# Loading the first weight block of a fused mixer kernel in column halves on two queues

## The chip, the cores and the metric

The kernel runs on one core of a Trainium2 chip. The metric is device time in microseconds (us). The kernel before takes 206.7 us (206.62 to 207.2 in three executions). In the views of the profile PE is TensorE, PEld its weight loads, DVE VectorE, ACT ScalarE, POOL GpSimd and SP SyncE; a trailing q marks a queue's issue of a load. A load has "landed" when its completion is signalled.

## The reference, cut to what matters

Two mixers work on the same `x` (2048 x 512) and are blended by a gate of each row. The change touches only the beginning of branch B: `x @ w_in`, of which the second half of the columns goes through a gelu and a layer norm.

```python
def _B_ref(x, w_in, w_sp, b_sp, w_out):
    z = _gelu(jnp.einsum('bsd,df->bsf', x, w_in))     # w_in is 512 x 1376
    z1 = z[..., :Fh].copy()
    z2 = _layernorm(z[..., Fh:], axis=-1)             # Fh = 688: the kernel starts here
    g = jnp.einsum('ts,bsf->btf', w_sp, z2) + b_sp[None, :, None]
    return jnp.einsum('bsf,fd->bsd', z1 * g, w_out)
g = _sigmoid((x * gate_w).sum(-1, keepdims=True))     # gate: one more column of z2's product
a = _A_ref(x, A_wqkv, A_w_phi, A_wo)                  # linear attention; ... cut
b = _B_ref(x, B_w_in, B_w_sp, B_b_sp, B_w_out)
return g * a + (1 - g) * b
```

## The kernel before

The 512 rows of `w_in` are four blocks of 128 rows; here "block 0" to "block 3" are their z2 columns (128 x 688 bf16, 172 KB each). SP and ACT each have a queue of loads.

```python
def load_z2w(eng, dt):
    eng.dma_start(out=w_z2[:, dt, 0:FH], in_=w_in_v[:, dt, FH:F])
nc.sync.dma_start(out=xs[:, 0, :], in_=x2[0:P, :])          # first two x tiles
nc.scalar.dma_start(out=xs[:, 1, :], in_=x2[P:2 * P, :])
load_z2w(nc.sync, 0)
load_z2w(nc.scalar, 1)
load_z2w(nc.sync, 2)
nc.scalar.dma_start(out=gaterow[0:NDT, :], in_=gate_w.rearrange("(dt p) -> dt p", p=P))
load_z2w(nc.sync, 3)
# ... cut
x_dma_T(2, 2)                    # first DMA transpose on SP: x tiles 2 and 3
# ... cut: w_z1 (2 loads), further x tiles (transposed), brow, wqkT (transposed)
for u in range(8):
    nc.sync.dma_start(out=wphi[us, :, us], in_=heads[u])    # needed by fold()
# ... cut: wv_sb (2 loads), wspT (transposed)
```

TensorE (PE) starts with warm-up matmuls on constants, transposes two x tiles, and then runs the z2 products of both tiles, in the order in which their blocks are expected.

```python
warm_up(6); warm_up(1, P)
# ... cut: eight transposes of x tiles 0 and 1, copies to xT
one(0, 0, 0)                 # one(tile, block, column half)
z_part(0, 0, HF, True)       # tile 0, block 0, second half
gate_T()                     # transposes gaterow; needs its load
one(0, 1, 0)                 # first use of block 1
one(1, 0, 0)
z_part(1, 0, HF, True)
one(1, 1, 0)
# ... cut: blocks 1 (second half), 2 and 3 of both tiles
```

The softmax here doesn't subtract the row's maximum and nothing guards it: scores larger than these inputs give would overflow.

## Time and profile before

| What | Where it is read | Value |
|---|---|---|
| span of the profiled execution | page | 204.5 us |
| PE busy | page, part 1 | 98% |
| first z matmul | timeline of PE | 4.53 us |
| block 1 issued / landed after | issues of the tile | 1.24 us / 3.4 us |
| first DMA transpose on SP issued | timeline of SP | 2.66 us |
| last `w_phi` load issued | timeline of SP | 23.96 us |
| fold, first to last matmul | timeline of PE | 25.93 to 26.41 us |

The page of the kernel before: busy us of each engine with its share of the span, and the engines of the chain of work that ended last.

```profile
PE 200.8 (98%) x1557; PEld 119.9 (59%) x1557; DVE 130.4 (64%) x283; ACT 74.8 (37%) x122; POOL 45.6 (22%) x76
...
PE 98%; DVE 0%; issue 0%
```

PE is the bound from end to end, so only a wait of PE can be won or lost. The timeline of PE around the first z matmuls (start us, length us, engine, line, operation, out<-in, count):

```profile
4.10 0.42 PE L280 MATMUL pq<-ident,xs 128*128 128x128 bf16 x2
4.53 0.44 PE L191 MATMUL zp<-w_z,xT 128*128 128x344 bf16 x1
4.77 0.38 PE L230 MATMUL zp<-w_z,xT 128*128 128x344 bf16 x1
4.99 0.17 PE L290 MATMUL pq<-ident,gaterow 128*128 128x4 bf16 x1
5.02 0.45 PE L191 MATMUL zp<-w_z,xT 128*128 128x344 bf16 x2
5.31 0.31 PE L230 MATMUL zp<-w_z,xT 128*128 128x344 bf16 x1
5.46 0.89 PE L191 MATMUL zp<-w_z,xT 128*128 128x344 bf16 x5
```

Look at the starts, for the lengths overlap. The last transpose starts at 4.21, and the first z matmul only at 4.53: about 0.2 us of waiting for block 0. From 5.02 on a z matmul starts each 0.145 us, without a gap.

The same time from the SP queue (timeline of SP; its rows are issues of loads), with the `w_phi` row far below:

```profile
0.81 0.39 SPq L119 DMA_DIRECT2D xs<-in_A_x_dram  x1
1.25 1.36 SPq L117 DMA_DIRECT2D w_z<-in_B_w_in_dram  x3
2.66 1.33 SPq L131 DMA_TRANSPOSE xT<-in_A_x_dram  x1
4.04 1.08 SPq L135 DMA_DIRECT2D w_z<-in_B_w_in_dram  x2
...
20.25 4.13 SPq L150 DMA_DIRECT2D wphi<-in_A_w_phi_dram  x8
```

SP issues without a pause: the transpose goes out the moment the load before it is issued. The last of the eight `w_phi` loads goes out at 23.96. It landed 1.6 us later, at 25.56, and the fold starts at 25.93:

```profile
25.93 0.56 PEld L307 LDWEIGHTS <-wqkT 32*128 32x128 bf16 x64 [0.28 <-issue]
```

That is no wait, but under 0.4 us of slack; I did not see this before I predicted. Two more views are compared below: the stretches from 3.5 to 4.5 us (last two columns: busy share of the DMA engines, which can pass 1 because a packet counts whole where it starts, and GB/s; before them the busy time of each engine and the granted clock), and the issue of block 1 with its time to landing.

```profile
3.50:4.00 0.50, 0.50 (x8) 0.50 (x7) 0.19 (x1) 0.32 (x2) 0.00 (x0) 1.00 0.97 302
4.00:4.50 0.50, 0.50 (x5) 0.36 (x4) 0.40 (x3) 0.00 (x0) 0.00 (x0) 1.00 0.98 312
```

```profile
L117 ACTq DMA_DIRECT2D w_z<-in_B_w_in_dram x1: 456/456/456, 1.2 to 1.2; - x1
...
DMA to landing us min/median/max: 3.4/3.4/3.4
```

### The profile page before, as it was taken

To read this page: it belongs to the slowest core of one execution; us is meant where nothing else is said; L and a number is where in the kernel's file an instruction comes from. 1 tells how busy PE (TensorE), PEld (TensorE's weight loads), DVE (VectorE), ACT (ScalarE), POOL (GpSimd) and SP (SyncE) were. 2 spreads that over 40 slices of the span, in tenths; PEclk is the share of its full clock that TensorE was granted. 3 is DMA by queue.
4 is the path that set the end of the run, shared out by engine and by line. 5 is a ranking of instruction groups with operands and counts; after the bars stand their busy time and mean duration, and the time that the engine had idled before them with its cause. 6 is when DMAs were issued, how large, how long until landed. Compare 5 with 4: busy or idle time off the path is not lost.

```text
span 204.5 us, 3996 instructions
## 1 busy us (share of the span) xinstructions
PE 200.8 (98%) x1557; PEld 119.9 (59%) x1557; DVE 130.4 (64%) x283; ACT 74.8 (37%) x122; POOL 45.6 (22%) x76
## 2 busy tenths in 40 slices
PE   8999999999999999999999999999999999999994
PEld 4666666655665555656565666555555555665642
DVE  4567484837977587979797789555566645633332
ACT  3566678796222333332424042222251136002303
POOL 3020202021523325334242442222204220200000
PEclk9999999999999999999999999999999999999999
DMA  6999699999999027940423219853567458552833
GB/s 194 252 205 171 80 151 290 146 278 247 256 249 213 3 38 182 287 94 16 75 48 45 51 38 120 154 109 64 105 161 80 90 113 183 63 96 51 156 64 104
DMA packets 89931, 27.22 MB, mean 133 GB/s; under 512 B 84184, under 2 KB 89912, under 8 KB 89912
## 3 DMA queue, kind: packets, MB, share of 16 engines
q1 hardware_dynamic: 87744, 24.99, 65.4%
q10 hardware_dynamic: 2168, 1.98, 3.5%
q8 instruction: 12, 0.20, 0.4%
q14 instruction: 7, 0.06, 0.1%
HBM read 4.15 MB, written 2.10 MB: 31 GB/s over the span
## 4 chain that ended last, share of the span: by engine, by line
PE 98%; DVE 0%; issue 0%
PE mm L454 37%; PE zp L191 18%; PE mm L355 14%; PE mm L515 9%; PE mm L509 7%; PE mm L395 7%; PE kvacc L411 2%; PE at L467 2%; PE zp L222 1%; PE mm L520 1%; PE zp L307 0%; PE pq L280 0%; PE at L478 0%; PE pq L307 0%; DVE ob L527 0%; PE zp L230 0%
## 5 line engine op out<-in xcount | busy, mean ns | idle before, releaser
L454 PE MATMUL mm<-z2all,wspT 128*128 128x344 bf16 x512 | 79.9, 309 | 0.0
L454 PEld LDWEIGHTS <-wspT 128*128 128x128 bf16 x512 | 49.0, 98 | 25.3
L191 PE MATMUL zp<-w_z,xT 128*128 128x344 bf16 (+1 forms) x254 | 38.1, 310 | 0.0
L359 ACT ACTIVATE eq<-mm 128x512 bf16<-128x512 f32 x32 | 17.4, 594 | 51.4 <-PE mm L355 25.7
L363 DVE TENSOR_REDUCE zs<-eq 128x64 f32<-128x1024 bf16 x16 | 19.5, 1220 | 20.0 <-ACT eq L359 20.0
L191 PEld LDWEIGHTS <-xT 128*128 128x128 bf16 x254 | 24.4, 98 | 11.8
L359 ACT ACTIVATE ek<-mm 128x512 bf16<-128x512 f32 x32 | 17.3, 600 | 27.1 <-PE mm L355 27.1
L459 DVE SCALAR_TENSOR_TENSOR ucat<-mm,bT,z1all 128x344 bf16<-128x344 f32 x32 | 17.4, 544 | 15.0 <-PE mm L454 15.0
L372 POOL TENSOR_TENSOR eq<-eq,ratio 128x512 bf16<-128x512 bf16 x16 | 16.9, 1055 | 44.6 <-DVE ratio L371 36.7
L531 ACT ACTIVATE ob<-mm,g_inv 128x512 bf16<-128x512 f32 (+1 forms) x15 | 10.1, 680 | 33.1 <-PE mm L520 28.5
L363 DVE TENSOR_REDUCE zs<-ek 128x64 f32<-128x1024 bf16 x16 | 19.3, 1209 | 2.8 <-ACT ek L359 2.8
L515 PE MATMUL mm<-wspT,uT 128*128 128x512 bf16 (+2 forms) x85 | 20.1, 367 | 0.0
L355 PEld LDWEIGHTS <-xT 128*128 128x128 bf16 x128 | 12.2, 98 | 12.0
L372 POOL TENSOR_TENSOR ek<-ek,ratio 128x512 bf16<-128x512 bf16 x16 | 16.9, 1056 | 2.2 <-DVE ratio L371 1.7
L509 PE MATMUL mm<-wspT,oT 128*128 128x512 bf16 (+2 forms) x68 | 16.6, 366 | 0.0
L355 PE MATMUL mm<-wq_p,xT 128*128 128x512 bf16 x64 | 16.4, 379 | 0.0
L395 PE MATMUL mm<-wv_sb,xT 128*128 128x512 bf16 x64 | 16.4, 379 | 0.0
L355 PE MATMUL mm<-wk_p,xT 128*128 128x512 bf16 x64 | 16.3, 379 | 0.0
L209 DVE BATCH_NORM_STATS2 bn<-z2all 128x6 f32<-128x344 bf16 x32 | 14.9, 501 | 0.0
L206 ACT ACTIVATE z2all<-zp 128x688 bf16<-128x688 f32 x16 | 11.8, 744 | 7.3 <-PE zp L191 7.2
L260 ACT ACTIVATE z1all<-zp 128x688 bf16<-128x688 f32 x16 | 11.9, 744 | 5.1 <-PE zp L191 4.6
L515 PEld LDWEIGHTS <-uT 128*128 128x128 bf16 x85 | 8.1, 98 | 9.4 <-issue 0.2
(77 smaller groups left out, 142.7 us busy)
## 6 DMA issues: line engine op xcount, KB each, us to landing
out_dram<-ob ACTq DMA_DIRECT2D x12, 128.0 KB, 2.4
wspT<-in_B_w_out_dram SPq DMA_DIRECT2D x2, 640.0 KB, 4.9
w_z<-in_B_w_in_dram SPq DMA_DIRECT2D x2, 344.0 KB, 4.7
w_z<-in_B_w_in_dram SPq DMA_DIRECT2D x3, 172.0 KB, 3.5
wv_sb<-in_A_wqkv_dram SPq DMA_DIRECT2D x2, 256.0 KB, 2.7
wspT<-in_A_wo_dram SPq DMA_DIRECT2D x2, 256.0 KB, 4.0
out_dram<-ob SPq DMA_DIRECT2D x3, 128.0 KB, 1.8
uT<-ucat SPq DMA_TRANSPOSE x16, 2.8
```

Of the source, the lines that this page charges most:

```text
L191: nc.tensor.matmul(zp[:, j, 0:n], lhsT=xT[:, dt, tt * P:(tt + 1) * P], rhs=wt[:, dt, j * HF:j * HF + n], start=(dt == 0), stop=(dt == NDT ...
L209: nc.vector.bn_stats(out=bn6[:, tt, j, :], in_=z2v[:, j, :])
L260: nc.scalar.activation(out=z1all[:, tt, :].rearrange("p (j n) -> p j n", j=2), in_=zp[:, :, 0:HF], func=AF.Gelu_apprx_tanh,)
L355: nc.tensor.matmul(ps[:, :], lhsT=xT[:, dt, tt * P:(tt + 1) * P], rhs=w[:, dt, :], start=(dt == 0), stop=(dt == NDT - 1))
L359: nc.scalar.activation(out=e[:, :, a, :], in_=ps[:, :].rearrange("p (h f) -> p h f", f=DH), func=AF.Exp, scale=1.0 - 2.0 * a)
L363: nc.vector.tensor_reduce(out=z[:].rearrange("p h a -> p (h a)"), in_=e[:].rearrange("p h a f -> p (h a) f"), axis=AX.X, op=ALU.add,)
L372: nc.gpsimd.tensor_tensor(out=e[:, :, 1, :], in0=e[:, :, 1, :], in1=ratio[:, :, None].to_broadcast([P, H, DH]), op=ALU.mult)
L395: nc.tensor.matmul(v_ps[:, :], lhsT=xT[:, dt, tt * P:(tt + 1) * P], rhs=wv_sb[:, dt, :], start=(dt == 0), stop=(dt == NDT - 1))
L454: nc.tensor.matmul(gp[:, 0:HF], lhsT=wspT[:, st, tt * P:(tt + 1) * P], rhs=z2all[:, st, j * HF:(j + 1) * HF], start=(st == 0), stop=(st == ...
L459: nc.vector.scalar_tensor_tensor(out=ucat[tt % NU][:, c0 + j * HF:c0 + (j + 1) * HF], in0=gp[:, 0:HF], scalar=bT[:, tt:tt + 1], in1=z1all[ ...
L509: nc.tensor.matmul(acc, lhsT=oTs[tt][:, g, :], rhs=wo_t[:, g, c0:c1], start=start and g == 0, stop=stop and g == NG - 1)
L515: nc.tensor.matmul(acc, lhsT=uTs[tt][:, i + ft, :], rhs=w_main[i][:, ft, c0:c1], start=start and ft == 0, stop=False)
```

## The change

Block 0 is cut into two column halves of 344, one on each queue right behind the x tiles, so that it no longer shares the engines with block 1 (in the kernel before they landed at 4.49 and 4.68 us, and from 3.5 to 4.0 us the SP queue moved 0.05 MB and the ACT queue 0.10). PE uses block 0 for both tiles before it needs the gate row and block 1. The two loads of `wv_sb` become one.

```diff
-    load_z2w(nc.sync, 0)
+    for eng, c in ((nc.sync, 0), (nc.scalar, HF)):
+        eng.dma_start(out=w_z2[:, 0, c:c + HF], in_=w_in_v[:, 0, FH + c:FH + c + HF])
     load_z2w(nc.scalar, 1)
@@
-    for h in range(2):
-        nc.sync.dma_start(
-            out=wv_sb[:, 2 * h:2 * h + 2, :],
-            in_=A_wqkv[h * 2 * P:(h + 1) * 2 * P, 2 * D:3 * D].rearrange("(dt p) n -> p dt n", p=P),
-        )
+    nc.sync.dma_start(out=wv_sb[:, :, :], in_=A_wqkv[:, 2 * D:3 * D].rearrange("(dt p) n -> p dt n", p=P))
@@
         one(0, 0, 0)
         z_part(0, 0, HF, True)
+        one(1, 0, 0)
+        z_part(1, 0, HF, True)
         gate_T()
         one(0, 1, 0)
-        one(1, 0, 0)
-        z_part(1, 0, HF, True)
         one(1, 1, 0)
```

## The prediction

> **What bounds the kernel now.** TensorE: the page gives PE 200.8 of 204.5 us busy (98%), and the chain that ended last is 98% PE. Only at the start can a load hold PE back, so all that the change can win lies in the first 5 us or so.
>
> **The start, from the timeline of the first 8 us.** PE warms up from 0.84 us, then runs eight transposes of two x tiles, one each 0.107 us (128 columns: half speed), the last starting at 4.21 and so feeding until about 4.32. The first z matmul starts at 4.53: the load of w_in block 0, issued at 1.25, took 3.2 us to land. So PE waits about 0.21 us for block 0. It runs the second z matmul at 4.77, the gate matmul at 4.99 (weight load at 4.92, just after gaterow lands), the next z at 5.02, and from there one z each 0.145 us without a gap. Full clock is recorded from 4.92 us on; the waited 0.21 us was half-speed time, worth about 0.10 us at full speed. That is the whole prize: 0.05% of 206.7 us.
>
> **What the change does to it.** In the DMA packet records, block 0 (SP queue) and block 1 (ACT queue) end at nearly the same time (last data 3.97 and 4.23 us): they share the engines[...]. So block 0 is there when about 600 KB have moved. After the change only 256 KB of x and 172 KB of block 0 come first: at some 300 GB/s (packet records of 2.25 to 4.25 us) about 0.5 us earlier, landing near 4.0 (estimate). The first z matmul is then released by the transposes, near 4.32.
>
> The price: block 1 and gaterow sit behind half of block 0 on the ACT queue, behind about 770 KB in all. Estimate: block 1 lands near 5.1 instead of 4.65, gaterow near 5.3 instead of 4.88. PE has four block-0 matmuls to cover this: two at half speed (4.32 to 4.90), two mostly at full speed, done at about 5.20. So the gate matmul stalls up to about 0.1 us, and block 1 is just in time. Sixth z matmul: before at 5.46; after at 5.40 to 5.50. Blocks 2 and 3 come at the same total of bytes as before, and land (5.26, 5.72) before they are needed (5.9, 6.5). Net: 0.0 to 0.1 us won.
>
> The merged load of wv_sb takes one 0.45 us issue from SP at 24.4 us; wv_sb is first used at 45.4. The order of DVE and GpSimd is unchanged; ACT gets one more issue before its table load, whose result is not needed before 7.03.
>
> **Predicted time: 206.6 us, 8 in 10 between 206.2 and 207.1.** Faster by over 2%: 0.01; within 2%: 0.98; slower by over 2%: 0.01.
>
> **What would show it.** Right: first z matmul at 4.3 to 4.4, no longer behind a load; gaterow named as the wait before the gate's weight load; block 1 landing 0.3 to 0.6 us later; the sixth z start within 0.1 us of before; the rest of the PE stream merely shifted. Wrong: block 0 landing after 4.4, or a gap over 0.2 us before the gate or block 1.
>
> **What would make it wrong.** The moment of full clock moves between executions[...]. A lost PE slot late in the kernel would also outweigh it.

The sum comes to 206.7 us less the 0.0 to 0.1 us won at the start, so 206.6. Half speed is what the traces have before the moment of full clock that they record (4.92 us before, 5.96 in the change): z matmuls start 0.29 us apart (4.36 to 4.65 in the change), and 0.145 us after it.

## More of the kernel before

The transposed loads of the later x tiles follow on SP, and far behind them the loads of `w_phi`.

`fold()` later multiplies the attention weights with `w_phi`, on PE, between two z tiles.

In the trace the SP and ACT loads signal their landing on eight semaphores in turn. The ninth load gets the first one's again, and this program makes it wait on it: in the kernel before that is a load of `w_z1`, which goes out at 4.04 us and waits for the load of x tile 1 (landed at 3.58).

## The result, and the profile after

The change takes 207.19 us in the median (206.97 to 207.85, 6 executions), the kernel before 206.66 us (206.58 to 207.2): a ratio of 1.0025, interval 1.0008 to 1.0042. Ratios here are the mean time of one kernel's fast runs over that of the other's of the same rounds, so not quite the ratio of the medians. It is slower clear of noise, by about 0.5 us, and the median is 0.09 us above the predicted range. A second timing (`after_again`, below) gave 207.07 us and again 1.0025. That 207.07 lies inside the predicted range is luck: the same waits are in its profile, and the forecast was a gain of 0.0 to 0.1 us.

The page after: PE is still nearly all of the chain, but loads have come into it.

```profile
PE 200.5 (97%) x1539; PEld 120.0 (58%) x1557; DVE 130.4 (63%) x283; ACT 74.7 (36%) x122; POOL 45.6 (22%) x76
...
PE 94%; DMA 2%; DVE 1%; issue 1%; ACTq 0%; ACT 0%
```

(The trace lacks 18 of the 1557 matmul records; they are missing, not idle.) The timeline of PE at the start of the change, with the wait and its releaser in brackets:

```profile
4.15 0.42 PE L277 MATMUL pq<-ident,xs 128*128 128x128 bf16 x2
4.36 0.49 PE L188 MATMUL zp<-w_z,xT 128*128 128x344 bf16 x1
4.65 0.49 PE L227 MATMUL zp<-w_z,xT 128*128 128x344 bf16 x1
4.94 0.49 PE L188 MATMUL zp<-w_z,xT 128*128 128x344 bf16 x1
5.22 0.49 PE L227 MATMUL zp<-w_z,xT 128*128 128x344 bf16 x1
5.83 0.18 PE L287 MATMUL pq<-ident,gaterow 128*128 128x4 bf16 x1
6.37 1.04 PE L188 MATMUL zp<-w_z,xT 128*128 128x344 bf16 x6 [0.35 <-DMA w_z<-in_B_w_in_dram]
```

The first z matmul starts at 4.36, right after the transposes, as intended. Four block-0 matmuls run. Then PE waits for gaterow until 5.83, and for block 1 until 6.37. In the kernel before the fifth and sixth z matmuls started at 5.31 and 5.46; here at 6.37 and 6.51. Block 1 took this long:

```profile
L117 ACTq DMA_DIRECT2D w_z<-in_B_w_in_dram x1: 454/454/454, 1.7 to 1.7; - x1
...
DMA to landing us min/median/max: 4.6/4.6/4.6
```

Issued at 1.73, landed at 6.33. Much had gone ahead of it. The DMA view up to block 1's last data (5.88 us; in the second profile of the change, `after_again`, 5.11 us) has the total and the two queues, q1 being SP's and q10 ACT's (the last line is the total of the second profile):

```profile
DMA packets 1324, 1.04 MB, mean 177 GB/s; under 512 B 435, under 2 KB 1324, under 8 KB 1324
q1 hardware_dynamic: 885, 0.64, 39.4%
q10 hardware_dynamic: 439, 0.40, 20.1%
...
DMA packets 993, 0.94 MB, mean 183 GB/s; under 512 B 122, under 2 KB 993, under 8 KB 993
```

In the first profile the trace also has fifteen of block 1's sixteen completion signals by 5.63 us and the last only at 6.33; in the second profile no such straggler. The engines also moved less from 3.5 to 4.5 us than before (302 and 312 GB/s there):

```profile
3.50:4.00 0.50, 0.50 (x7) 0.47 (x6) 0.14 (x1) 0.50 (x1) 0.00 (x0) 1.00 0.88 208
4.00:4.50 0.50, 0.50 (x7) 0.50 (x5) 0.41 (x3) 0.32 (x2) 0.00 (x0) 1.00 0.88 267
```

And the SP queue has a pause that was not there before:

```profile
1.73 0.90 SPq L117 DMA_DIRECT2D w_z<-in_B_w_in_dram  x2
3.71 1.33 SPq L132 DMA_TRANSPOSE xT<-in_A_x_dram  x1
5.08 1.08 SPq L136 DMA_DIRECT2D w_z<-in_B_w_in_dram  x2
...
22.59 3.81 SPq L151 DMA_DIRECT2D wphi<-in_A_w_phi_dram  x8
```

The loads before it are issued by 2.63, but the transpose goes out at 3.71 (2.66 before). The compiled program says why. This is SP's queue of the change (a listing of the program, not a profile):

```
1 L119 DMACopy xs<-in_A_x_dram 128x512
2 L122 DMACopy w_z_69<-in_B_w_in_dram 128x344
3 L117 DMACopy w_z_69<-in_B_w_in_dram 128x688 x2
4 L132 DmaTransposeAnt xT<-in_A_x_dram 128x4x256 [waits DMAHW0_49]
```

With one load more ahead of it, the transpose is the ninth and gets the first semaphore again, on which this program makes it wait: that of ACT's load of x tile 1. Before, the transpose was the eighth and waited for nothing. In the trace x tile 1 landed at 3.69 us, and the transpose goes out at 3.71 (second profile: 3.52 and 3.54). The rest of SP's queue starts about 1 us later. At the fold, PE now waits for `w_phi` (timeline of the weight loads):

```profile
26.98 0.10 PEld L304 LDWEIGHTS <-wqkT 32*128 32x128 bf16 x3 [0.28 <-DMA wphi<-in_A_w_phi_dram]
27.68 0.56 PEld L304 LDWEIGHTS <-wqkT 32*128 32x128 bf16 x61 [0.61 <-DMA wphi<-in_A_w_phi_dram]
```

One can add this up by landmarks of the timelines. The table gives each moment in us, and in brackets how far it is behind the kernel before. It has runs that come below.

| Profile | first gelu of z2 | first gelu of z1 | last fold matmul | first exp of k |
|---|---|---|---|---|
| before | 7.03 | 10.82 | 26.41 | 45.95 |
| change | 8.08 (+1.05) | 11.88 (+1.06) | 28.16 (+1.75) | 47.59 (+1.64) |
| change, second profile | 7.49 (+0.46) | 11.61 (+0.79) | 27.38 (+0.97) | 46.81 (+0.86) |
| `lane_only` | 6.98 (-0.05) | 11.11 (+0.29) | 26.76 (+0.35) | 46.19 (+0.24) |
| `lane_again` | 7.13 (+0.10) | 10.93 (+0.11) | 27.98 (+1.57) | 47.40 (+1.45) |
| `halves_sp` | 7.44 (+0.41) | 11.24 (+0.42) | 28.05 (+1.64) | 47.51 (+1.56) |
| `halves01` | 7.00 (-0.03) | 10.80 (-0.02) | 26.50 (+0.09) | 45.92 (-0.03) |

After the fold nothing more is lost: the spans of the two profiles of the change, 206.1 and 205.3 us, are 1.6 and 0.8 us over the 204.5 of before, as the last column says. (The profile of before fell on one of its faster executions, 206.2 us, and the first of the change on its slowest, 207.85 us, so these differences are larger than the 0.5 us of the medians. The second profile, of a 207.06 us execution, is the more usual one.)

### The profile page after: what moved, and what is told of

Read it like the earlier page. It is cut to its first block, busy times and chain, and to the rows that moved or that the text cites. A ratio compares the mean times of both kernels' runs of the same rounds, so it can differ in the third digit from the quotient of the medians.

```text
span 206.1 us, 3978 instructions
## 1 busy us (share of the span) xinstructions
PE 200.5 (97%) x1539; PEld 120.0 (58%) x1557; DVE 130.4 (63%) x283; ACT 74.7 (36%) x122; POOL 45.6 (22%) x76
## 4 chain that ended last, share of the span: by engine, by line
PE 94%; DMA 2%; DVE 1%; issue 1%; ACTq 0%; ACT 0%
PE mm L451 36%; PE zp L188 18%; PE mm L352 13%; PE mm L512 8%; PE mm L392 7%; PE mm L506 7%; DMA w_z<-in_B_w_in_dram 2%; PE kvacc L408 2%; PE at L464 2%; PE mm L517 1%; DVE bn L206 0%; ACT z2all L203 0%; PE zp L304 0%; PE at L475 0%; PE pq L304 0%
## 5 line engine op out<-in xcount | busy, mean ns | idle before, releaser
L506 PE MATMUL mm<-wspT,oT 128*128 128x512 bf16 (+2 forms) x61 | 15.6, 364 | 0.4
```

What stands on the lines that cost most here:

```text
L506: nc.tensor.matmul(acc, lhsT=oTs[tt][:, g, :], rhs=wo_t[:, g, c0:c1], start=start and g == 0, stop=stop and g == NG - 1)
```

## The experiments

Theories. **G**: block 1 and gaterow are late behind half of block 0, and PE waits for them. **L**: the ninth load waits for a semaphore, the SP queue is late, and PE waits later, at the first z1 tile and at the fold. **H**: a gap in PE's work at the start delays the full clock. All kernels gave correct results. "before" is the kernel before in the same rounds.

### First round: the parts one by one

`reorder_only`: the loads of before, the matmul order of the change.

> The loads of the kernel before, the matmul order of the change (gate matmul after the four block-0 matmuls of both tiles). All theories: nothing, within 0.1 us of before (206.66), because block 1 lands at 4.65 us and is never waited for. If the reorder alone cost time, the ratio would be over 1.001.

Measured: 206.26 us (206.11 to 206.78), before 206.43; ratio 0.9995, interval 0.9979 to 1.0011. The order alone does nothing that this timing can show.

`halves_only`: the change with the matmul order of before.

```diff
-        one(1, 0, 0)
-        z_part(1, 0, HF, True)
         gate_T()
         one(0, 1, 0)
+        one(1, 0, 0)
+        z_part(1, 0, HF, True)
```

> The loads of the change, the matmul order of before. Theory L ([...]the first DMA transpose on SP is the ninth and must wait for the first x load; the SP queue then runs about 1 us late and the fold waits for w_phi): same as the change, +0.4 to +0.7 us over before, fold wait 0.3 us or more. Theory G (block 1 and gaterow late behind half of block 0 is all of the loss): slower than the change, by another 0.1 to 0.4 us, because the gate matmul comes after two matmuls instead of four.

Measured: 207.90 us (207.14 to 209.24); ratio 1.0086, interval 1.0053 to 1.0118. Worse than the change, as G said: PE runs two matmuls, then waits from 5.06 to 6.63 us for gaterow. So the new order hides part of what the new loads cost. The fold did not wait in this profile, PE being later than SP.

`lane_only`: before, with one more tiny load that nobody reads.

```diff
+    pad = early.tile([P, P], BF16, name="pad")
     nc.scalar.dma_start(out=gaterow[0:NDT, :], in_=gate_w.rearrange("(dt p) -> dt p", p=P))
+    nc.scalar.dma_start(out=pad[0:NDT, :], in_=gate_w.rearrange("(dt p) -> dt p", p=P))
```

> The kernel before with one more tiny load (a second copy of gate_w, 1 KB, into a tile that nobody reads) on the ACT queue ahead of the first DMA transpose; block 0 is whole and the matmul order is that of before. Theory L: first DMA transpose of SP issued at 3.5 to 3.7 us instead of 2.66, the whole SP stream 0.8 to 1.0 us late, the fold waits for w_phi for 0.3 to 1 us, time +0.3 to +0.9 us. Theory G: no change in time, within 0.1 us.

Measured: 207.32 us (206.54 to 207.92); ratio 1.0040, interval 1.0019 to 1.0061. One load of 1 KB costs about what the change does, or more (the intervals overlap). The transpose went out at 3.47. Its profile fell on its fastest execution: PE waits 0.28 us for block 1 at 4.98, but full clock came early (3.71 us) and the first gelu is not late; what it loses, it loses at the first z1 tile, and no fold wait of 0.3 us is there. Therefore it was run again below.

`after_gate_pool`: the change with gaterow on the GpSimd queue. In its compiled program this load signals on none of the eight semaphores.

```diff
-    nc.scalar.dma_start(out=gaterow[0:NDT, :], in_=gate_w.rearrange("(dt p) -> dt p", p=P))
+    nc.gpsimd.dma_start(out=gaterow[0:NDT, :], in_=gate_w.rearrange("(dt p) -> dt p", p=P))
```

> The change with gaterow loaded from the GpSimd queue, so that it neither queues behind block 1 nor takes one of the eight semaphores of the SP and ACT loads. Theory L: first DMA transpose again at about 2.7 us, no fold wait, time back to 206.5 to 206.8. Theory G: only the wait at the gate goes, block 1 is as late as before, 206.9 to 207.1.

Measured: 207.70 us (207.08 to 209.16); ratio 1.0076, interval 1.0044 to 1.0108. Neither theory had this. The transpose went out at 2.68 and the fold did not wait, as L said, but block 1 was as late as ever, and two of six executions took 209.08 and 209.16 us, the profiled one among them. Its timeline of PE:

```profile
5.61 0.21 PE L287 MATMUL pq<-ident,gaterow 128*128 128x4 bf16 x1
6.51 1.88 PE L188 MATMUL zp<-w_z,xT 128*128 128x344 bf16 x6 [0.69 <-DMA w_z<-in_B_w_in_dram]
...
8.26 0.74 PE L188 MATMUL zp<-w_z,xT 128*128 128x344 bf16 x2
```

After the gap, six matmuls take 1.88 us, where the same six took 1.04 us in the change: still half speed. The clock records of this trace have full clock from 9.99 us on; before had it from 4.92. This is theory H. It is not shown which gaps do this: the change itself, whose PE is idle about as long before its block 1 (0.8 us in all, an estimate from the starts between 5.22 and 6.37 us), has full clock from 5.96, in the middle of it.

### Second round: block 1 in time, fillers, `w_phi` elsewhere

`after_fill`: the change with three useless matmuls where it waits.

```diff
+        fill = pq_tile([P, CH])
+        for _ in range(3):
+            nc.tensor.matmul(fill[:, :], lhsT=nc.const_aps.tensor(1.0, [P, P], BF16),
+                             rhs=nc.const_aps.tensor(1.0, [P, CH], BF16), start=True, stop=True)
         gate_T()
```

> The change with three filler matmuls (128x512, constant operands, a scratch bank) ahead of the gate matmul, where the change waits for gaterow and block 1. They do no useful work. Theory G alone (the wait for block 1 is the whole loss): same as the change, +0.5 us over before, or up to 0.5 us slower. Theory H[...]: no execution over 208.3 us.

Measured: 207.60 us (207.53 to 207.84), before 206.54 (205.94 to 208.53); ratio 1.0047, interval 1.0013 to 1.0081. No slow tail, but none of the change's own executions was over 207.85 either, and one of before was at 208.53. So nothing points to H as a part of the change's usual loss.

`w1_halves`: the change with block 1 in column halves on both queues too, and blocks 2 and 3 as one load, so that the transpose is still the ninth load.

```diff
+    for dt in range(2):
+        for eng, c in ((nc.sync, 0), (nc.scalar, HF)):
+            eng.dma_start(out=w_z2[:, dt, c:c + HF], in_=w_in_v[:, dt, FH + c:FH + c + HF])
+    nc.sync.dma_start(out=w_z2[:, 2:4, 0:FH], in_=w_in_v[:, 2:4, FH:F])
```

> The change with block 1 also loaded in column halves by both queues, and blocks 2 and 3 as one load so that the first DMA transpose on SP is still the ninth load and still waits for the first x load. Theory G: block 1 lands near 4.7 to 5.0 us instead of 6.3, no wait over 0.1 us at block 1, time 206.4 to 206.9 (0 to +0.4 over before, what is left being the late SP queue). Theory L: +0.4 us or more over before as in the change.

Measured: 206.90 us (206.78 to 207.48); ratio 1.0017, interval 0.9979 to 1.0056, unclear. The halves of block 1 landed at 5.48 and 5.65, later than the expected 4.7 to 5.0, and cost PE under 0.1 us; block 2 and the first z1 tile cost 0.19 us each. Of the forms of the change that still load block 0 first it has the lowest ratio, and it does not beat before.

`balanced`: `w1_halves` with gaterow on the GpSimd queue.

> As w1_halves, and gaterow from the GpSimd queue, so that only seven loads precede the first DMA transpose and it waits for none. If late block 1 and the late SP queue are the whole loss, both are gone: equal to before within 0.1 us, or better by up to 0.1 us. If it is still 0.4 us slower, something else costs the time.

Measured: 207.16 us (206.85 to 207.28); ratio 1.0021, interval 0.9987 to 1.0055. The expectation failed: the transpose went out at 2.68, but the joint load of blocks 2 and 3 landed at 6.89 us, and PE waited 0.68 us for it. Not a clean test of "both removed".

`after_wphi_pool`: the change with the `w_phi` loads on the GpSimd queue.

```diff
-        nc.sync.dma_start(out=wphi[us, :, us], in_=heads[u])
+        nc.gpsimd.dma_start(out=wphi[us, :, us], in_=heads[u])
```

> The change with the eight w_phi loads issued from the GpSimd queue instead of SP at 22 to 26 us, so that the fold of the attention weights can not wait for them. If the fold wait (0.6 us in the profile of the change) is part of the usual loss: faster than the change by 0.2 to 0.6 us. If it is in the profiled execution alone: same as the change.

Measured: 208.34 us (207.63 to 209.28); ratio 1.0083, interval 1.0040 to 1.0127. A miss: these loads now go out in the first us and crowd the start (gaterow at 6.66 us, a PE gap from 5.47 to 6.70). Three of six executions took over 209 us; in the profile full clock comes at 10.24 us. So it does not answer its question, but it is a good subject for H.

### Third round: why block 1 is late, and theory H

`after_again`: the change once more.

> The change once more, as the control of this call. Expected: 0.2 to 0.6% slower than before; in its profile block 1 lands at 5.9 to 6.5 us, the first gelu of z2 starts 0.5 to 1.2 us later than in before's profile (7.03), and every later stage is merely shifted by that. If the fold wait for w_phi (0.6 us in the first profile) comes again, theory L has a part in the usual loss; if not, it was of that execution.

Measured: 207.07 us (206.83 to 207.53), before 206.68; ratio 1.0025, interval 1.0005 to 1.0045. Block 1 landed at 5.57, a little before the expected 5.9, and gaterow at 5.58. The timeline of PE shows the wait at the gate, and, where the SP queue is late, the wait at the first z1 tile:

```profile
5.62 0.18 PE L287 MATMUL pq<-ident,gaterow 128*128 128x4 bf16 x1 [0.41 <-DMA gaterow<-in_gate_w_dram]
...
10.83 0.60 PE L188 MATMUL zp<-w_z,xT 128*128 128x344 bf16 x3 [0.17 <-DMA w_z<-in_B_w_in_dram]
```

By the table of landmarks: 0.46 us lost at the start, 0.33 at the first z1 tile, some 0.1 to 0.2 at the fold.

`rows_split`: block 0 in row halves instead of column halves.

```diff
+    for eng, r in ((nc.sync, halves[0]), (nc.scalar, halves[1])):
+        eng.dma_start(out=w_z2[r, 0, 0:FH], in_=w_in_v[r, 0, FH:F])
```

> The change, but block 0 split into row halves (partitions 0 to 63 by SP, 64 to 127 by ACT, rows of 1376 B) instead of column halves (rows of 688 B). Same bytes, same places in both queues. Theory P (block 1 is late because of its place in the queue and because both queues turn to a new load at once): block 1 lands at 5.8 to 6.5 us, as slow as the change. Theory R (the half rows slow the engines): the packet rate between 3.5 and 4.5 us is back at 300 GB/s, block 1 lands near 5.1, 0 to 0.2 us over before.

Measured: 208.37 us (207.58 to 208.58); ratio 1.0075, interval 1.0049 to 1.0100. Block 0 itself came only at 5.15 and 5.39 us, full clock at 8.77. This way of cutting it did not help; 328 GB/s from 4.0 to 4.5 us, but 184 from 3.5 to 4.0.

`halves_sp`: both column halves of block 0 on SP, block 1 and gaterow at their old places on ACT.

```diff
-    for eng, c in ((nc.sync, 0), (nc.scalar, HF)):
+    for eng, c in ((nc.sync, 0), (nc.sync, HF)):
```

> The change, but both column halves of block 0 on the SP queue, one after the other, so that block 1 and gaterow keep their places of before on the ACT queue. Nine loads precede the DMA transpose as in the change. Theory P: block 1 lands at 4.6 to 5.0 us, no wait over 0.15 us at gate or block 1, 0 to 0.5 us over before (what is left is the late SP queue at the first z1 tile, as in the run with one more load). Theory R: block 1 lands after 5.5 us and the time is that of the change.

Measured: 208.11 us (207.70 to 210.17); ratio 1.0088, interval 1.0052 to 1.0123. Block 1 landed at 4.39, even before the 4.6 to 5.0 of theory P, the second half of block 0 at 4.66 and gaterow at 4.20; but the time did not follow. In this profile the fold waits 0.9 us at one matmul, and ends 1.64 us later than before. Of this, 0.41 us is lost at the start: about 0.1 in a wait for the second half of block 0, the rest by the clock (full at 5.60 instead of 4.92; half of that is 0.34, an estimate). The other 1.2 us is the late SP queue.

`wphi_fill`: `after_wphi_pool` with the three fillers.

> The variant with w_phi on the GpSimd queue, half of whose executions took 209.0 to 209.3 us, with the three filler matmuls ahead of the gate matmul. Theory H[...]: no execution over 208.4 us, all within about 0.5 us of 207.7. If 209 us executions remain, they are not from the gap.

Measured: 207.99 us (207.71 to 208.28); ratio 1.0066, interval 1.0047 to 1.0086. No execution near 209 any more, where three of six were. The fillers do no useful work, so this supports H: those executions lost their time to the gap. It does so by the times alone, for in the profiled execution PE is at full speed before the gap (z matmuls at 4.33 and 4.47).

### Fourth and fifth round: both causes away

`halves_sp_pool`: `halves_sp` with gaterow on the GpSimd queue.

> halves_sp (both column halves of block 0 on the SP queue, block 1 at its old place on ACT) with gaterow from the GpSimd queue: seven SP and ACT loads precede the first DMA transpose, which waits for none. If late block 1 and the late SP queue are the whole loss: DMA transpose at about 2.7 us, block 1 at 4.6 to 5.0, no wait over 0.15 us at the first z1 tile or the fold, time within 0.2 us of before (halves_sp was 1.4 us slower). If it stays 0.5 us or more slower, a cause is missing.

Measured: 207.71 us (207.43 to 209.47), before 206.50; ratio 1.0080, interval 1.0051 to 1.0108. Again not clean: PE waits about 0.9 us at the second half of block 0, which landed at 5.45 (at 4.66 in `halves_sp`, from the same place on SP; why is not shown), SP has five loads to issue so that its transpose goes out at 3.16, and the fold waits 0.4 us.

`lane_pool`: `lane_only` with the extra load on the GpSimd queue.

```diff
-    nc.scalar.dma_start(out=pad[0:NDT, :], in_=gate_w.rearrange("(dt p) -> dt p", p=P))
+    nc.gpsimd.dma_start(out=pad[0:NDT, :], in_=gate_w.rearrange("(dt p) -> dt p", p=P))
```

> The kernel before with the same extra 1 KB load as lane_only, but from the GpSimd queue. If the semaphore wait is what cost lane_only 0.9 us: DMA transpose at 2.66 us, time within 0.2 us of before. If the extra load itself disturbs the start: about as slow as lane_only.

Measured: 206.53 us (206.31 to 207.01); ratio 1.0001, interval 0.9988 to 1.0014. The same extra load costs nothing that this timing can show when it does not push the transpose to ninth place; the transpose goes out at 2.66:

```profile
2.66 1.33 SPq L133 DMA_TRANSPOSE xT<-in_A_x_dram  x1
```

`before_gate_pool`: before with gaterow on the GpSimd queue.

> The kernel before with gaterow from the GpSimd queue. A control: within 0.2 us of before. If it is slower, the GpSimd queue costs something of its own and the two runs beside it are to be read with that.

Measured: 207.01 us (206.57 to 207.23); ratio 1.0023, interval 1.0011 to 1.0035. Not the free control that I expected: the gate matmul starts at 5.42 instead of 4.99 in its profile, so this queue brought gaterow later here (5.37 against 4.88). In the profiles of the three variants with gaterow there PE did not wait for it (landed at 5.05, 4.57 and 5.39, used at 5.61, 5.50 and 5.92), so this does not explain their losses.

`halves01`: blocks 0 and 1 together in column halves, one load on each queue, with the rest of the change. Seven loads come before the transpose, as in the kernel before.

```diff
-    for eng, c in ((nc.sync, 0), (nc.scalar, HF)):
-        eng.dma_start(out=w_z2[:, 0, c:c + HF], in_=w_in_v[:, 0, FH + c:FH + c + HF])
-    load_z2w(nc.scalar, 1)
+    for eng, c in ((nc.sync, 0), (nc.scalar, HF)):
+        eng.dma_start(out=w_z2[:, 0:2, c:c + HF], in_=w_in_v[:, 0:2, FH + c:FH + c + HF])
```

> Blocks 0 and 1 together loaded in column halves, one load on each queue, with the matmul order of the change and its merged wv load. Seven loads precede the DMA transpose, as in before, and block 1 comes with block 0. If late block 1 and the ninth load are the whole loss: DMA transpose at 2.66 us, both blocks at 4.4 to 4.9, time within 0.2 us of before. If half rows on both queues slow the start by themselves: blocks after 5.3 us, 0.3 us or more slower.

Measured: 207.05 us (206.21 to 207.06), before 206.62; ratio 1.0010, interval 0.9990 to 1.0030. The time alone is unclear: the interval holds both no loss and the change's 1.0025, and four of the six executions took 207.05 us. The profile, which fell on the fastest execution (206.21 us), is the clean test of the waits. Timeline of SP, and the stretches from 3.5 to 4.5 us:

```profile
2.71 1.32 SPq L131 DMA_TRANSPOSE xT<-in_A_x_dram  x1
```

```profile
3.50:4.00 0.50, 0.50 (x8) 0.50 (x7) 0.19 (x1) 0.40 (x2) 0.00 (x0) 1.00 1.10 334
4.00:4.50 0.50, 0.41 (x6) 0.24 (x4) 0.44 (x3) 0.10 (x1) 0.00 (x0) 1.00 1.08 372
```

The blocks landed at 4.41 and 4.64, the engines moved 334 and 372 GB/s with half rows on both queues, and every landmark is within 0.1 us of before. So half rows did not slow the engines here, and neither wait of the change appears.

`lane_again`: `lane_only` a second time.

> lane_only once more. Theory L: again 0.5 to 1.0 us slower than before, and the waits in its profile are at the first z1 tile (0.3 us, block of w_in for z1 late) and at the fold (w_phi late, 0.2 us or more), none over 0.2 us before 8 us.

Measured: 207.91 us (207.41 to 208.30, 4 executions); ratio 1.0064, interval 1.0038 to 1.0090. This time the profile shows the loss, and at the fold alone (timelines of SP and of the weight loads):

```profile
3.65 1.33 SPq L133 DMA_TRANSPOSE xT<-in_A_x_dram  x1
```

```profile
26.50 0.09 PEld L309 LDWEIGHTS <-wqkT 32*128 32x128 bf16 x1 [0.37 <-DMA wphi<-in_A_w_phi_dram]
27.50 0.56 PEld L309 LDWEIGHTS <-wqkT 32*128 32x128 bf16 x61 [0.91 <-DMA wphi<-in_A_w_phi_dram]
```

The start is 0.10 us behind before, the end of the fold 1.57 us. The last `w_phi` load went out at 25.78 instead of 23.96.

## Why the prediction was wrong

- **What bounds the kernel, and the prize at the start:** right. The first z matmul moved from 4.53 to 4.36 (second profile 4.32); block 0 landed at 3.89 and 4.07 where the estimate was 4.0. The predicted gain of the early start is there and is worth about 0.1 us.
- **"So the gate matmul stalls up to about 0.1 us, and block 1 is just in time":** wrong, a term of the sum that was mis-sized. Block 1 was to land near 5.1 and gaterow near 5.3. They landed at 6.33 and 5.79 in one profile, 5.57 and 5.58 in the other. The sixth z matmul, predicted for 5.40 to 5.50, started at 6.51 and 5.81. The term that failed is "behind about 770 KB in all" (0.79 MB). The assumed 300 GB/s was less wrong: from 3.5 to 4.0 us the change moved 208 and 238 GB/s in its two profiles, where before moved 302, but 0.80 MB had still been moved by 4.83 and 4.63 us, and the prediction needed this near 4.65 (its 5.1 less the 0.45 us that block 1 took in before from its last data to landing). Block 1's last data, however, came only after 1.04 and 0.94 MB: SP's queue went on to block 3 meanwhile (and, in the first profile, to the transpose) and was ahead of ACT's, 0.64 and 0.54 MB against 0.40. At 300 GB/s the excess over 0.79 MB is 0.8 and 0.5 us (estimates), most of the 1.2 and 0.5 us by which block 1 was late. With this the start loses 0.5 to 1.0 us instead of gaining 0.1.
- **"The rest of the PE stream merely shifted":** wrong, and here a step was missing altogether. I counted bytes and issue times of the added load, but not its semaphore. As one load more ahead of SP's first transpose it makes that transpose wait for x tile 1 on ACT (3.71 us instead of 2.66), and SP runs about 1 us late. I had also not asked how much slack the later users of SP's queue have, having written "Only at the start can a load hold PE back": it is 0.37 us at the fold, from 25.56 to 25.93. `lane_only`, `lane_again` and `lane_pool` show that this alone costs 0.4 to 0.6%.
- **How the two meet:** they do not add up, since a PE that is late anyway waits less for a late SP. In `halves_only` PE was so late that the fold did not wait; in `halves_sp` and `lane_again`, where PE's start was less late (0.41 and 0.10 us), the fold added 1.2 and 1.5. The change has some of both: 1.05 at the start and 0.70 at the fold in one profile; 0.46, 0.33 and some 0.2 in the other.
- **The clock:** the warning that the moment of full clock moves was right; what such a move costs was not in the sum. One kernel had it at 3.71 and 5.32 us (`lane_only`, `lane_again`). Among the profiles with no wait over 0.4 us in PE's start, full clock came from 3.71 us (`lane_only`) to 6.56 us (`lane_pool`). The first gelu of `lane_pool`, which has no wait that before lacks, is 0.82 us behind that of before, half of the 1.64 us by which its full clock is later. So one profile of each kernel can't settle a difference of 0.5 us by its span; the waits inside it can.

What is shown and what is not. Shown: without the ninth load and without a late block 1, the profile with halved loads has neither wait (`halves01`; whether its time is that of before stays unclear at this size); the ninth load alone costs time (`lane_again` against `lane_pool`); block 1 and gaterow come late in both profiles of the change, and PE waits for them. Open: why SP's queue gets ahead of ACT's, why one of sixteen shares of block 1 came 0.7 us after the others in the first profile, and why the engines move less from 3.5 to 4.5 us when whole blocks 1 and 2 follow on the two halves of block 0. Half rows alone do not explain the last (`halves01`), and cutting by rows does not cure it (`rows_split`). Also open: which gaps in PE's work delay the full clock, and why SP's queue loses another 1 us between 11 and 18 us in some executions (in the first profile of the change the `brow` load takes 1.84 us to issue, in the second 0.51). And no version beat the kernel before clear of noise.

## What to carry to other kernels

Before you add a load, count the loads ahead of every queue's next one: here, with eight semaphores used in turn, one load more made an unrelated load wait for the first (3.47 and 3.65 us instead of 2.66 with one 1 KB load), and that load cost about as much as the whole change, or more (ratios 1.0040 and 1.0064 against 1.0025). When a load is moved forward, ask what it pushes back, what the other queue moves meanwhile, and whether the matmuls that are to cover this are long enough. And a kernel whose PE is 98% busy can still have a second chain with no slack beside it: look for the latest load before each first use, not only for waits.
